# Adding all head dims' products on VectorE, with part of the additions moved to accumulating DMA, in a fused attention and token-MLP kernel

## The chip, the cores and the metric

One core of one Trainium2 chip. The metric is device time in microseconds (us) of one execution. The span of a profile is the time from the first to the last instruction of that execution; device time is a little longer than the span. Every run told below was fast, where not said otherwise.

The engines are named as the profile names them: PE (matmul), PEld (its weight loads), DVE (VectorE), ACT (ScalarE), POOL (GpSimd), SP (the queue that issues most DMAs).

## The reference

The output mixes two branches by a gate per row: `g * a + (1 - g) * b`, with `g = sigmoid(sum(x * gate_w))`, S = 2048 rows and D = 512 columns, bf16.

```python
# branch a: 32 heads of 16 dims; each row attends to 8 rows: itself and 2, 4, ... 14 rows back
logits = einsum("bhsd,bhswd->bhsw", q, kg) * Dh**-0.5      # masked where the row is below 0
attn   = softmax(logits, axis=-1)
o      = einsum("bhsw,bhswd->bhsd", attn, vg);  a = o @ wo
# branch b: an MLP over rows (tokens)
h = layernorm(x);  u = gelu(einsum("bsd,sf->bdf", h, w1) + b1);  y = einsum("bdf,fs->bds", u, w2) + b2
```

## The kernel before

Heads and four groups of head dims lie on the 128 partitions, so a sliding window is a shifted view along the free axis. For each half of the rows (h = 0, 1) DVE multiplies q by eight shifted views of k, for each of four groups `dl` of head dims. The products are summed pairwise on DVE into two buffers; PE then sums the rest with a 0/1 matrix (`RP`, 128 x 32) in one burst of small matmuls that reads both buffers. Softmax runs on DVE and ACT; GpSimd's DMA queue spreads the weights over the head dims ("attention copies"); DVE multiplies by V and adds the eight window places in three steps.

```python
def f_sum(h, b0, b1, with_gate):                 # one burst on PE
    ...                                          # 16 gate matmuls when h == 0
    for wp in range(4):
        for k_, b_ in enumerate((b0, b1)):       # two buffers: 32 matmuls
            for c in range(4):
                ins = e.matmul(ps[32*c:32*c+32, 4+wp, :], lhsT=RP,
                               rhs=sub(PB[b_], 2*wp*HS + c*UT_, [(HS, 2), (1, UT_)]),
                               start=(k_ == 0), stop=(k_ == 1), tile_position=(0, 32*c))
...
for h in range(2):
    for pr in range(2):
        ...                                      # two products into bb[0], bb[1]
        A("dve", tt(PB[bb[0]], PB[bb[0]], PB[bb[1]], ALU.add), ...)
...
for u in range(8):                               # AV, 256 rows each
    A("dve", tt(pv, <V, shifted>, <weights>, ALU.mult), ...)             # 128x8192
    A("dve", tt(pv[:, 0:4], pv[:, 0:4], pv[:, 4:8], ALU.add), ...)       # 128x4096
    A("dve", tt(pv[:, 0:2], pv[:, 0:2], pv[:, 2:4], ALU.add), ...)       # 128x2048
    A("dve", tt(OT[:, u], pv[:, 0], pv[:, 1], ALU.add), ...)             # 128x1024
...
MLPB = [0, 1, 2, 0, 1, 2, 3, 0, 1, 2, 3, 4, 5, 6]    # PSUM bank of each of 14 token-MLP tiles
```

PE's work is one chain in a fixed order: Q, K, V projections; the first MLP product (224 matmuls, "ph2") with the two sum bursts put in; the second MLP product ("ph3") with the output projection of `a` ("wo") added five tiles behind. A list scheduler in the kernel, with its own estimates, orders each engine's instructions when the program is built.

## Time and profile before

| | before |
|---|---|
| device time, median of the first 3 runs | 171.63 us (171.59 to 172.5) |
| profiled execution: device time, span | 170.61 us, 168.5 us |
| PE busy, DVE busy | 161.6 us, 151.9 us |
| PE's first wait of size: for the last V eviction, near 48 us | 0.69 us |
| PE's last wait: for DVE's last AV result | 1.04 us (0.82, see below) |

First the page of the kernel before: the span, then each engine's busy time with its share of the span.

```profile
span 168.5 us, 2085 instructions
...
PE 161.6 (96%) x835; PEld 79.4 (47%) x851; DVE 151.9 (90%) x115; ACT 73.1 (43%) x102; POOL 19.6 (12%) x57
```

The next lines are the waits of before (who waited for whom: us in total, times, longest).

```profile
DVE arena L688 <- DMA arena<-in_A_x_dram: 7.5, 3, 5.2
...
PE ps L841 <- DVE arena L446: 1.0, 1, 1.0
...
DVE arena L446 <- PE ps L719: 0.8, 1, 0.8
PE ps L805 <- ACT arena L449: 0.8, 2, 0.7
```

L841 is the output projection: PE waits for DVE once, at the very end. L688 are the layer norm's statistics, which wait for rows of x at the start. The third line shows that DVE in turn once waits for PE (L719 is the sum burst). The timeline of PE shows where (start us, us, engine, line, shapes; in brackets the idle time before and what ended it):

```profile
9.74 3.40 PE L649 MATMUL ps<-arena 128*128 128x512 bf16 x15
...
48.65 7.08 PE L805 MATMUL ps<-arena 128*128 128x512 bf16 x31 [0.69 <-ACT arena L449]
...
56.53 1.90 PE L719 MATMUL ps<-arena 128*32 128x512 bf16 x32
58.59 6.85 PE L805 MATMUL ps<-arena 128*128 128x512 bf16 x31 [0.16 <-issue]
...
88.23 1.91 PE L719 MATMUL ps<-arena 128*32 128x512 bf16 x32
90.30 1.67 PE L805 MATMUL ps<-arena 128*128 128x512 bf16 x7 [0.16 <-issue]
92.13 10.53 PE L805 MATMUL ps<-arena 128*128 128x512 bf16 x47 [0.15 <-ACT arena L449]
...
159.51 3.62 PE L841 MATMUL ps<-arena 128*128 128x512 bf16 x16
164.18 1.69 PE L841 MATMUL ps<-arena 128*128 128x512 bf16 x11 [1.04 <-DVE arena L446]
```

After the second burst there is one more wait, of 0.15 us for ACT, which evicts the sums. The gap of 0.16 us behind each burst, in which PE seems to wait for nothing, is no wait. This profile holds 851 weight loads but only 835 matmuls: 16 matmuls have no record. Two of them are the first matmuls behind the two bursts (hence x31 and x7, not x32 and x8; the first one's weight load is there, at 58.36 us). In the profile of a1_before, the same program run again (see the experiments), all 851 are there, and the gap is not:

```profile
PE 163.0 (97%) x851; PEld 79.4 (47%) x851; DVE 151.9 (90%) x115; ACT 73.1 (43%) x102; POOL 19.5 (12%) x57
...
56.67 1.90 PE L719 MATMUL ps<-arena 128*32 128x512 bf16 x32
58.51 7.08 PE L805 MATMUL ps<-arena 128*128 128x512 bf16 x32
...
164.09 1.91 PE L841 MATMUL ps<-arena 128*128 128x512 bf16 x12 [0.82 <-DVE arena L446]
```

So from its start to the start of the next matmul a burst takes 1.84 us (56.67 to 58.51). The last wait is 0.82 us: the line of 1.04 above lacks the first of its twelve matmuls. And the durations of DVE's large operations, kept apart by shape (busy us, mean ns of one):

```profile
L446 DVE TENSOR_TENSOR arena<-arena 128x8192 bf16<-128x8192 bf16 x16 | 70.7, 4420 | 1.8 <-DMA arena<-arena 0.9 <-PE ps L719 0.8
L446 DVE TENSOR_TENSOR arena<-arena 128x4096 bf16<-128x4096 bf16 x16 | 36.4, 2288 | 0.2
```

### The profile page before, as it was taken

What the parts mean: (1) busy time and instruction counts of PE and PEld (TensorE: products, weight loads), DVE (VectorE), ACT (ScalarE), POOL (GpSimd) and SP (SyncE); (2) the same over time, 40 slices, a digit from 0 to 9 for tenths busy, and PEclk for the clock granted to TensorE, in tenths of its full rate; (3) what the DMA queues carried; (4) which work ended last, traced back from release to release, by engine and by line L of the source; (5) the groups of instructions that cost most, each with busy time, mean ns of one, the idle gap of its engine ahead of it and who ended that gap; (6) DMA issues with size and microseconds to landing.
All of it is one profiled execution on the core that took longest, in us unless ns stands there. A gap on an engine that the chain in (4) does not pass through costs nothing.

```text
span 168.5 us, 2085 instructions
## 1 busy us (share of the span) xinstructions
PE 161.6 (96%) x835; PEld 79.4 (47%) x851; DVE 151.9 (90%) x115; ACT 73.1 (43%) x102; POOL 19.6 (12%) x57
## 2 busy tenths in 40 slices
PE   6999999999989999999999999999999999999973
PEld 2865555555534444444443444444444444444732
DVE  2609999999999799999979999999999999999981
ACT  3266777666671277656215297000121111111172
POOL 7000000000000000000396000079100000000000
PEclk9999999999999999999999999999999999999999
DMA  5999999910000392995799999999900011000022
GB/s 137 271 247 252 235 321 290 302 66 6 0 0 0 110 302 63 285 286 142 215 218 288 355 275 270 290 243 207 198 31 31 31 46 51 31 31 31 31 91 96
DMA packets 43144, 26.87 MB, mean 159 GB/s; under 512 B 7552, under 2 KB 41984, under 8 KB 43136
## 3 DMA queue, kind: packets, MB, share of 16 engines
q1 hardware_dynamic: 40800, 21.96, 49.9%
q0 software_dynamic: 1632, 4.21, 10.4%
q10 hardware_dynamic: 704, 0.59, 1.1%
q8 instruction: 6, 0.10, 0.3%
q14 instruction: 2, 0.02, 0.0%
HBM read 18.88 MB, written 2.10 MB: 125 GB/s over the span
## 4 chain that ended last, share of the span: by engine, by line
PE 54%; DVE 36%; ACT 4%; issue 3%; DMA 2%; DVEq 0%
DVE arena L446 36%; PE ps L805 24%; PE ps L649 22%; ACT arena L449 3%; PE ps L590 2%; PE ps L719 2%; DMA arena<-in_A_x_dram 2%; PE ps L841 1%; PE ps L569 1%; ACT L901 1%; PE ps L713 1%; PE ps L560 1%; DVE arena L881 0%; DVEq L905 0%; PE ps L779 0%
## 5 line engine op out<-in xcount | busy, mean ns | idle before, releaser
L446 DVE TENSOR_TENSOR arena<-arena 128x8192 bf16<-128x8192 bf16 (+10 forms) x72 | 134.8, 1902 | 3.2 <-DMA arena<-arena 0.9
L832 PE MATMUL ps<-arena 128*128 128x512 bf16 (+1 forms) x234 | 50.0, 366 | 0.2
L805 PE MATMUL ps<-arena 128*128 128x512 bf16 x218 | 48.7, 379 | 1.4 <-ACT arena L449 0.8
L449 ACT ACTIVATE arena<-ps,arena 128x512 bf16<-128x512 f32 (+1 forms) x30 | 21.6, 728 | 65.2 <-PE ps L841 46.6
L449 ACT ACTIVATE arena<-ps 128x512 bf16<-128x512 f32 (+3 forms) x53 | 33.4, 649 | 20.3 <-PE ps L649 10.4
L649 PE MATMUL ps<-arena 128*128 128x512 bf16 x172 | 38.0, 379 | 0.2
L832 PEld LDWEIGHTS ps<-arena 128*128 128x128 bf16 x238 | 23.3, 98 | 25.3
L805 PEld LDWEIGHTS ps<-arena 128*128 128x128 bf16 x224 | 21.5, 98 | 28.2 <-ACT arena L449 1.8
L649 PEld LDWEIGHTS ps<-arena 128*128 128x128 bf16 x176 | 19.8, 113 | 17.7
L771 POOL DMA_DIRECT2D arena<-arena x32 | 16.4, 517 | 98.3 <-DVE arena L446 98.3
L688 DVE BATCH_NORM_STATS2 arena<-arena 128x6 f32<-128x512 bf16 x16 | 10.0, 682 | 7.5 <-DMA arena<-in_A_x_dram 7.5
L841 PE MATMUL ps<-arena 128*128 128x512 bf16 (+1 forms) x66 | 15.5, 366 | 1.1 <-DVE arena L446 1.0
L901 ACT ACT_TABLE_LOAD x9 | 11.5, 1283 | 2.4 <-issue 2.3
L841 PEld LDWEIGHTS ps<-arena 128*128 128x128 bf16 x68 | 6.6, 98 | 8.2 <-DVE arena L446 1.3
L449 ACT ACTIVATE arena<-arena 128x16 f32<-128x16 f32 (+5 forms) x10 | 6.8, 679 | 5.2 <-DVE arena L446 5.1
L702 DVE TENSOR_SCALAR arena<-arena 128x512 bf16<-128x512 bf16 x16 | 5.3, 413 | 0.0
L590 PE MATMUL ps<-arena 128*128 128x256 bf16 x32 | 3.8, 273 | 0.0
L719 PE MATMUL ps<-arena 128*32 128x512 bf16 x64 | 3.8, 380 | 0.0
L590 PEld LDWEIGHTS ps<-arena 128*128 128x128 bf16 x32 | 3.4, 114 | 0.4 <-DVE arena L580 0.4
L543 PE MATMUL ps<-arena 128*128 128x512 bf16 x5 | 2.3, 628 | 1.1 <-POOL arena L455 1.1
L719 PEld LDWEIGHTS ps<-arena 128*32 128x32 bf16 x64 | 1.6, 97 | 1.9 <-issue 0.4
L881 DVE TENSOR_SCALAR arena<-ps,arena 128x256 bf16<-128x256 f32 x1 | 0.5, 544 | 2.0 <-PE ps L841 2.0
(36 smaller groups left out, 15.3 us busy)
## 6 DMA issues: line engine op xcount, KB each, us to landing
arena<-in_B_w_dram SPq DMA_DIRECT2D x7, 1024.0 KB, 8.3
arena<-in_B_w_dram SPq DMA_DIRECT2D x8, 896.0 KB, 7.9
arena<-arena POOLq DMA_DIRECT2D x32, 128.0 KB, 4.3
out_dram<-arena SPq DMA_DIRECT2D x15, 128.0 KB, 1.7
arena<-in_A_x_dram SPq DMA_DIRECT2D x3, 512.0 KB, 4.3
arena<-in_A_wqkv_dram SPq DMA_DIRECT2D x2, 512.0 KB, 5.9
arena<-in_A_wo_dram SPq DMA_DIRECT2D x1, 512.0 KB, 8.7
arena<-in_A_x_dram SPq DMA_DIRECT2D x2, 128.0 KB, 3.4
```

What stands on the lines that cost most here:

```text
L446: return lambda e: e.tensor_tensor(out=o_, in0=a_, in1=b_, op=op_)
L449: return lambda e: e.activation(out=o_, in_=i_, func=f_, **kw)
L590: ins = e.matmul(ps[:, dl, hb * 256:hb * 256 + 256], lhsT=sub(WQKV, dt * 3 * D + dl, [(4, 128)]), rhs=XT[:, dt, hb * 256:hb * 256 + 256], ...
L649: ins = e.matmul(ps[:, bank, :], lhsT=sub(WQKV, dt * 3 * D + tn * D + dl, [(4, 128)]), rhs=XT[:, dt, sb * 512:(sb + 1) * 512], start=(dt = ...
L688: A("dve", (lambda t_: lambda e: e.bn_stats(out=ST6[:, t_, :], in_=X[:, t_, :]))(t), 0.67, reads=["x%d" % t], writes=["st%d" % t], name="s ...
L702: A("dve", (lambda t_: lambda e: e.tensor_scalar(out=X[:, t_, :], in0=X[:, t_, :], scalar1=col(RSTD, t_), scalar2=col(NMR, t_), op0=ALU.mu ...
L719: ins = e.matmul(ps[32 * c:32 * c + 32, 4 + wp, :], lhsT=RP, rhs=sub(PB[b_], 2 * wp * HS + c * UT_, [(HS, 2), (1, UT_)]), start=(k_ == 0), ...
L771: prev = sch.dma("pool", (lambda d_, s_: lambda e: e.dma_start(d_, s_))(dst, src), 131072, ds, issue=1.0, reads=["att%d" % h], writes=["av ...
L805: ins = e.matmul(ps[:, bank, :], lhsT=W1W[:, (ft // 2) % 3, st, 128 * (ft % 2):128 * (ft % 2) + 128], rhs=X[:, st, :], start=(st == 0), st ...
L832: ins = e.matmul(ps[:, bank, 0:c1 - c0], lhsT=W2S[i // 2][:, ft, 128 * (i % 2):128 * (i % 2) + 128], rhs=UT[:, ft, c0:c1], start=(ft == 0) ...
L841: ins = e.matmul(ps[:, bank, 0:c1 - c0], lhsT=OT[:, i // 2, dl, 128 * (i % 2):128 * (i % 2) + 128], rhs=WO[:, dl, c0:c1], start=False, sto ...
L901: e.preload_act_table_set(want)
```

## The change

The intent: let each sum burst read one buffer, so that PE has half as many small matmuls; DVE then has to add all four head-dim groups, and to make room on DVE, five additions (two of the pair additions of the first half, three of the eight first additions of AV) are done by DMAs that accumulate into their destination. The rest makes that fit: half-buffers laid out flat (s_ = 0, 1), a third AV buffer, another home for one W2 tile and for the output staging, plain loads of x ahead of the transposing ones, two of the first Q evictions on DVE, the W1 tiles 1 and 2 held back until the second accumulation has landed, the 32 attention copies merged into 8, and a new order of PSUM banks for the MLP.

```diff
             for k_ in range(1, 4):
+                ld_x(4 * k_, 4)
                 ld_xt(k_)
-                ld_x(4 * k_, 4)
...
-            evac(0, dl, 0, dl)
+            evac(0, dl, 0, dl, "act" if dl % 2 == 0 else "dve")
...
                 for wp in range(4):
-                    for k_, b_ in enumerate((b0, b1)):
-                        for c in range(4):
-                            ins = e.matmul(... rhs=sub(PB[b_], ...), start=(k_ == 0), stop=(k_ == 1), ...)
+                    for c in range(4):
+                        ins = e.matmul(... rhs=sub(PB[b0], ...), start=True, stop=True, ...)
...
+            def qaddd(x_, y_, s_, h=h):
+                o_, i_ = (sub(PB[b_], s_ * 4096, [(1, 4096)]) for b_ in (x_, y_))
+                qkd[h, s_] = sch.dma("pool", lambda e: e.dma_start(o_, i_, accum_op=ALU.add, max_dma_last_dim=4096), ...)
+            for s_ in range(2):
+                qk(0, bb[0], s_)
+                qk(1, bb[1], s_)
+                (qaddd if h == 0 else qadd)(bb[0], bb[1], s_)
+            ...
+            for s_ in range(2):
+                qadd(bb[0], bb[2], s_)
...
-                for dhi in range(4):             # 16 attention copies of 128 KB per half
+                src = psub(ATT[h], 32 * c, 32, 0, [(0, 4), (1, NW * UT_)])     # 4 of 512 KB
...
+        late_dep[0] = [qkd[0, 1]]
+        ld_w1(1); ld_w1(2)
...
+        AVD = (3, 4, 5)                          # AV units whose first addition is a DMA
...
-        MLPB = [0, 1, 2, 0, 1, 2, 3, 0, 1, 2, 3, 4, 5, 6]
+        MLPB = [1, 2, 0, 1, 2, 0, 3, 1, 2, 0, 3, 1, 2, 0]
```

(Priorities, buffer names and the ring of banks of ph3 change too.)

## The prediction

> **What bounds it now.** The page gives PE 161.6 us busy of 168.5 (96%), DVE 151.9 (90%), full granted clock. The two run neck and neck. The chain of waits runs on PE until about 92 us, then through ACT (log eviction, table load, exp) into DVE, which from 99.7 to 163.9 us never pauses (timeline). PE has little slack: it reaches the last output projection at 163.1 and waits 1.04 us for it (waits of PE on DVE). A gain needs both engines shortened.
>
> **Removed, added, moved (durations from the trace).**
> - PE: each sum burst goes from 32 small matmuls to 16. A burst takes 1.87 us (88.30 to 90.17 in the chain), so about 0.9 us less each, 1.8 us in all.
> - PE: the first token-MLP matmul waits 0.69 us for the last V eviction; the new bank order starts elsewhere: about 0.6 us less.
> - DVE, QK: before, 8 half-size products (2.29 us), 4 full-size products and 4 full-size additions (4.42 us): 53.7 us. After: 26 half-size operations, 59.5 us: +5.8 us.
> - DVE, AV: three half-size additions go to DMA: -6.9 us. Two Q evictions come over from ACT: about +1.4 us. So DVE's total is unchanged (+0.3 us).
> - DVE gains at the start: it idles 5.25 us, 7.6 to 12.8 us, waiting for x rows (waits). With plain loads ahead of the transposing ones the statistics start near 10.4 us. I count 3 us less idle: DVE finishes near 161.
> - Cost at the start: the second DVE Q eviction stands behind four statistics (4 x 0.62 us); PE's small bias transposes want its bank at 13.1 us and would wait about 0.5 us.
> - DMA: five accumulating transfers of 1 MB source each. [...] My estimate: the 32 software-queue copies move 4.2 MB in 10.4% of 16 engines' span, about 240 GB/s[...]. The order of instructions leaves about 9 us before DVE needs the second QK one and the first AV one. This is the tightest spot.
>
> **Critical path.** PE's arrival at the last projection: 163.1 - 1.8 - 0.6 + 0.5 = 161.2 us. DVE's finish about 161. The 1.04 us wait mostly vanishes: the end moves from 168.5 to about 165.5 us. Off 171.63 that is 168.6; I add a little for slips of the accumulating DMAs.
>
> **Prediction: 168.8 us, 80% range 167.5 to 171.0.** Faster by over 2%: 0.27; within 2%: 0.70; slower by over 2%: 0.03.
>
> **What would show it.** Sum bursts near 0.9 us each; no eviction wait near 48 us; DVE busy near 152 us with less idle before 13 us; layer norm done near 30 us, not 33; sum burst 0 near 54 and burst 1 near 92 us; accumulating DMAs landing in 8 to 10 us; the last PE wait under 0.5 us.
>
> **What would make it wrong.** Accumulating DMAs of 12 us or more: DVE stalls before its fourth products and the delayed AV additions, sum burst 0 holds PE, and the gain shrinks to 1 us or none. Their traffic delaying weight loads (two W1 loads now wait for the second accumulation). Transposing loads landing later and stalling projections near 13 or 21 us. On the good side: if the evictions and loads at the start cost PE nothing, 167.5.

With them the forecast for 1 MB came to about 9 to 11 us from issue to landing, where "What would show it" says 8 to 10: the author's estimate.

## The result, and the profile after

The changed kernel took 166.95 us (median of 4 runs, 166.47 to 167.41) against 171.61 (4 runs). The ratio is 0.9721, 95% interval 0.9683 to 0.9758: faster by 2.8%. A ratio here is formed from the fast runs of both kernels in the same rounds, so it is not quite the ratio of the medians quoted. The time lies 0.55 us below the predicted range, and over the 2% line that had been given a chance of 0.27.

| | before | after |
|---|---|---|
| device time, median | 171.61 us | 166.95 us |
| span of the profiled execution | 168.5 us | 165.3 us |
| PE busy, DVE busy | 161.6, 151.9 us | 159.8, 150.9 us |
| K projections start on PE | 9.74 us | 10.54 us |
| sum bursts start | 56.53 and 88.23 us | 54.74 and 92.30 us |
| last DVE result for PE | 163.9 us | 159.2 us |

The page of the changed kernel:

```profile
span 165.3 us, 1999 instructions
...
PE 159.8 (97%) x803; PEld 78.8 (48%) x819; DVE 150.9 (91%) x124; ACT 69.7 (42%) x98; POOL 13.7 (8%) x38
```

The waits of the changed kernel that answer to those shown of before (the line numbers have moved: L687 are the statistics, L892 the output projection, L717 the sum burst):

```profile
DVE arena L687 <- DMA arena<-in_A_x_dram: 3.7, 4, 1.8
...
PE ps L567 <- DMA arena<-in_A_x_dram: 0.8, 2, 0.7
...
DVE arena L445 <- DMA arena<-arena: 0.2, 1, 0.2
```

PE no longer waits for DVE anywhere. DVE waits for PE at the start (2.1 us, for the Q projections that it now evicts) and before the last instruction, and no more at the bursts. What is left of PE's waits after its first microsecond is one for an x tile at the start (L567). All five accumulating DMAs together make DVE wait 0.2 us. The timeline of PE of the changed kernel:

```profile
10.54 3.40 PE L648 MATMUL ps<-arena 128*128 128x512 bf16 x15
...
48.59 5.34 PE L856 MATMUL ps<-arena 128*128 128x512 bf16 x23
...
54.74 1.04 PE L717 MATMUL ps<-arena 128*32 128x512 bf16 x16
55.71 7.08 PE L856 MATMUL ps<-arena 128*128 128x512 bf16 x31
...
92.30 1.05 PE L717 MATMUL ps<-arena 128*32 128x512 bf16 x16
93.30 7.07 PE L856 MATMUL ps<-arena 128*128 128x512 bf16 x31
...
157.22 5.35 PE L892 MATMUL ps<-arena 128*128 128x512 bf16 x27
```

The wait before the MLP is gone (48.59). The first burst takes 0.97 us to the start of the next matmul (54.74 to 55.71), about half as long as before. The output projections run through to the end without a wait. DVE's large operations:

```profile
L445 DVE TENSOR_TENSOR arena<-arena 128x4096 bf16<-128x4096 bf16 x31 | 69.5, 2287 | 0.1
L445 DVE TENSOR_TENSOR arena<-arena 128x8192 bf16<-128x8192 bf16 x8 | 35.2, 4420 | 0.0
```

The 31 half-size operations add up to 69.5 us busy, not to 31 times their mean (70.9): neighbours overlap by some 0.05 us on average. And the accumulating DMAs of 1 MB each, issued at L742 (QK) and L825 (AV), first the two QK ones (time from issue to landing: shortest, median, longest), then the three AV ones, which were issued 4.3 us apart:

```profile
DMA to landing us min/median/max: 7.9/7.9/8.0
```

```profile
DMA to landing us min/median/max: 8.6/10.3/12.5
```

**The sum, from the K projections' start to PE's end.** Before, PE's stretch runs from 9.74 to 165.87 us (164.18 + 1.69), after from 10.54 to 162.57 us (157.22 + 5.35): 156.1 against 152.0, so 4.1 us less. (In both profiles the record of the first of these matmuls is missing, which moves both starts alike, by 0.22 us.) I count every part from the start of one matmul to the start of the next, in profiles or stretches where no record is missing. Without a wait this step is 0.22 us, but the record of a matmul is 0.38 us long, so neighbours overlap: a wait costs 0.16 us more than the idle time that the profile shows. The two bursts give 1.7 us (1.84 each in a1_before, 0.97 here). The eviction wait gives 0.86 (shown: 0.69) and the last wait 0.98 (shown in a1_before: 0.82). Two stops of PE in the MLP's first product give 0.49: 0.31 behind the second burst (shown: 0.15), and 0.18 near 72 us, where one step takes 0.39 us and no wait is shown. Together that is about 4.05. Which part of the change removed these two stops no run separates. The span fell by only 3.2 us because this one profile of the changed kernel started its K projections 0.8 us later. That the profile's span of 165.3 us agrees with the predicted 165.5 is thus partly luck, and the experiments had to separate the two.

### The profile page after: what moved, and what is told of

It is laid out like the page before. It is cut to its first block, busy times and chain, and to the rows that moved or that the text cites. A ratio compares the mean times of both kernels' runs of the same rounds, so it can differ in the third digit from the quotient of the medians.

```text
span 165.3 us, 1999 instructions
## 1 busy us (share of the span) xinstructions
PE 159.8 (97%) x803; PEld 78.8 (48%) x819; DVE 150.9 (91%) x124; ACT 69.7 (42%) x98; POOL 13.7 (8%) x38
## 4 chain that ended last, share of the span: by engine, by line
PE 93%; DMA 3%; issue 1%; ACTq 1%; DVE 0%
PE ps L856 29%; PE ps L883 29%; PE ps L648 23%; PE ps L892 8%; DMA arena<-in_A_x_dram 3%; PE ps L588 2%; PE ps L717 1%; PE ps L712 1%; ACTq L487 1%; DVE arena L932 0%; PE ps L567 0%; PE ps L797 0%; PE ps L661 0%; PE ps L663 0%; PE ps L662 0%
## 5 line engine op out<-in xcount | busy, mean ns | idle before, releaser
L445 DVE TENSOR_TENSOR arena<-arena 128x4096 bf16<-128x4096 bf16 (+9 forms) x79 | 131.9, 1720 | 1.2 <-DMA arena<-arena 0.2
L448 ACT ACTIVATE arena<-ps 128x512 bf16<-128x512 f32 (+3 forms) x51 | 32.7, 647 | 20.0 <-PE ps L648 11.1
L892 PE MATMUL ps<-arena 128*128 128x512 bf16 (+1 forms) x66 | 15.3, 366 | 0.1
L687 DVE BATCH_NORM_STATS2 arena<-arena 128x6 f32<-128x512 bf16 x16 | 10.1, 682 | 3.7 <-DMA arena<-in_A_x_dram 3.7
L785 POOL DMA_DIRECT2D arena<-arena x8 | 4.4, 563 | 75.2 <-DVE arena L445 75.2
L892 PEld LDWEIGHTS ps<-arena 128*128 128x128 bf16 x68 | 6.7, 98 | 7.2
L825 POOL DMA_DIRECT2D arena<-arena x3 | 3.6, 1200 | 17.7 <-DVE arena L445 17.7
L742 POOL DMA_DIRECT2D arena<-arena x2 | 2.5, 1234 | 30.3 <-DVE arena L698 21.6
## 6 DMA issues: line engine op xcount, KB each, us to landing
arena<-arena POOLq DMA_DIRECT2D x8, 512.0 KB, 11.2
```

What stands on the lines that cost most here:

```text
L445: return lambda e: e.tensor_tensor(out=o_, in0=a_, in1=b_, op=op_)
L448: return lambda e: e.activation(out=o_, in_=i_, func=f_, **kw)
L687: A("dve", (lambda t_: lambda e: e.bn_stats(out=ST6[:, t_, :], in_=X[:, t_, :]))(t), 0.67, reads=["x%d" % t], writes=["st%d" % t], name="s ...
L785: prev = sch.dma("pool", (lambda d_, s_: lambda e: e.dma_start(d_, s_))(dst, src), 524288, sch.dsem("av%d_%d" % (h, c)), issue=1.0, reads= ...
L825: sch.dma("pool", (lambda o_, i_: lambda e: e.dma_start(o_, i_, accum_op=ALU.add, max_dma_last_dim=4096))(pw(0, 4), pw(4, 4)), 1800000, sc ...
L892: ins = e.matmul(ps[:, bank, 0:c1 - c0], lhsT=OT[:, i // 2, dl, 128 * (i % 2):128 * (i % 2) + 128], rhs=WO[:, dl, c0:c1], start=False, sto ...
```

## The experiments

All had five rounds. Numbers are medians, with the ratio to the kernel before in the same rounds. Where "pinned" is said, each engine's instruction order was fixed to that of the kernel named, since the scheduler otherwise moves other work as well. I checked that pinning alone gives instruction for instruction the same program; that check is not among the runs on record. "PE's stretch" is the one of the sum above, from the first recorded K projection to PE's end.

### a1_before: the kernel before, run again

No edit.

> The kernel before, unchanged, run again so that each timed execution also shows its span. Open question: the profile of before had a span of 168.5 us and a device time of 170.61, while its timed runs gave 171.5 to 172.5; the changed kernel's profile (165.3, 166.99) agrees with its timed runs. Theory A (span varies): ordinary executions of before have spans of 169.4 to 170.5, that is the profile on record was a fast draw. Theory B (overhead outside the span): spans stay at 168.5 and time minus span is about 3.1 us for before against 1.7 us for after.

Measured: 170.89 us (6 runs); the 11 runs of before beside it gave 171.46 us. Spans ran from 168.6 to 169.8 us; time minus span was 2.1 to 2.3 us, mean 2.2. So both theories are half right. Executions of before differ by over 1 us in span, and the profile (168.5) was one of the shortest. Besides, before spends about 0.45 us more outside the span than the changed kernel (mean 1.7 us).

### a2_oldload: the old load order in the changed kernel, scheduler free

```diff
-                ld_x(4 * k_, 4)
                 ld_xt(k_)
+                ld_x(4 * k_, 4)
```

> The changed kernel with the loads of before (transposing load first, plain rows of x after it). Theory: the new load order makes the fourth x tile land late and costs PE 0.65 to 0.8 us at 7.4 us; undone, PE starts the K projections at 9.7 instead of 10.5 us, and since DVE finished 2 us before PE needed its last output, DVE's later start costs at most part of that: time 166.2 to 166.8, a ratio to before of about 0.968 to 0.971. Rival (the early loads are worth what they were meant for, because DVE is a co-bottleneck): DVE's layer norm ends at 33 instead of 31 us, PE waits at a sum burst or at the end, time 167.5 to 169.

Measured: 168.84 us, ratio 0.9841 (0.9801 to 0.9881). My theory of the late x tile was not borne out: the wait for it is gone here, but PE's K projections started at 10.31 us all the same (10.32 in the changed kernel, once its missing first record is allowed for), since the first Q projections ran slowly (below). The main loss was elsewhere, in a wait of PE for the last of the first MLP's weight tiles, since the scheduler had moved other things:

```profile
PE ps L856 <- DMA arena<-in_B_w_dram: 1.6, 1, 1.6
```

What does vary at the start shows in two profiles' timelines, the same eight matmuls first in this run, then in the changed kernel's:

```profile
5.70 1.71 PE L588 MATMUL ps<-arena 128*128 128x256 bf16 x8
```

```profile
5.53 1.06 PE L588 MATMUL ps<-arena 128*128 128x256 bf16 x8
```

Eight matmuls of 256 columns take 1.71 us in one and 1.06 in the other. Why the eight ran more slowly in one is not shown: the granted clock of both runs reads 1.0 as a mean of the whole run. And other profiles lost time at the start to first DMAs that landed late (0.65 us in the changed kernel's profile, for x), so the slow pace explains only part of the spread of spans.

### a3_dveadds: the five accumulations back on DVE

```diff
-                (qaddd if h == 0 else qadd)(bb[0], bb[1], s_)
+                qadd(bb[0], bb[1], s_)
-        AVD = (3, 4, 5)
+        AVD = ()
```

(The held-back W1 loads then wait for the matching DVE addition.)

> The changed kernel with all five accumulating DMAs replaced by the same additions on VectorE. Theory: DVE gets 5 x 2.29 = 11.4 us more, its end moves from 159.2 to about 170.6 and PE waits for it: time about 175 to 177, slower than before by about 2 to 3%. Rival (PE bounds the kernel and DVE has room): time within 1 us of the changed kernel, 167 to 168.

Measured: 177.57 us, ratio 1.0365 (1.0335 to 1.0395): 10.6 us more than the changed kernel and slower than before, as the theory had it; the time is 0.6 us above the stated range. The timeline of PE of this run shows the wait:

```profile
169.60 3.53 PE L895 MATMUL ps<-arena 128*128 128x512 bf16 x12 [6.75 <-DVE arena L445]
```

Without the accumulating DMAs the change would be a loss: PE's saving needs room on DVE, and they make it. The twelve matmuls after the wait also take 3.53 us, where the same twelve take 1.91 us in a1_before after a wait of 0.82 us. The granted clock of this run was 1.00 from 150 to 160 us and 0.77 in the mean from 160 to 175 us, the stretch that holds the wait and the twelve matmuls. After its wait of 6.75 us PE restarted slowly here. So some 1.6 us of the loss (3.53 against 1.91) are slow matmuls, not waiting. The scheduler was free in this run.

### a4_twobuf: bursts from two buffers again, without the final pair additions

```diff
-                    for c in range(4):
-                        ins = e.matmul(... rhs=sub(PB[b0], ...), start=True, stop=True, ...)
+                    for k_, b_ in enumerate((b0, b2)):
+                        for c in range(4):
+                            ins = e.matmul(... rhs=sub(PB[b_], ...), start=(k_ == 0), stop=(k_ == 1), ...)
...
-            for s_ in range(2):
-                qadd(bb[0], bb[2], s_)
```

> The changed kernel with the sum bursts reading two buffers again (no final pair additions on VectorE: 9.2 us less for DVE; 32 more small matmuls on PE: 1.8 us more). Theory (PE's stream alone bounds the changed kernel): bursts 1.8 us each again, time 168.5 to 169.0. Rival (DVE still bounds): DVE is 9 us shorter, so the time falls below 166.

Measured: 172.35 us over all six runs, two of them slow; the four fast ones had 170.82 to 172.97 and a ratio of 1.002 (0.9974 to 1.0066). Both theories missed. DVE was shorter, so the accumulating DMAs came earlier (120.0, 124.4 and 128.7 us instead of 127.7, 132.1 and 136.4) and ran beside the last weight loads. Of the last three loads of 896 KB one took 21.8 us to land, and the last, issued at 120.2 us, took 27.7; the last two have a median of 32.0, which puts the other near 36.3. The median of all such loads of the changed kernel is 10 us. Four attention copies, issued from 106.4 us on, landed there too, after 11.2 us in the median. The last load landed near 147.9 us (120.2 + 27.7), and an output DMA, issued behind it on the same queue at 131.8 us, at 148.3. The chain of waits of this run's profile (start us, us, what):

```profile
131.78 16.49 DMA out_dram<-arena
...
148.36 0.79 ACT arena L448
...
149.19 1.04 PE ps L882 x2
```

One output DMA of 128 KB took 16.5 us, its staging buffer was not free for ACT, and PE waited 4.6 us. Only this profile, of a slow run, shows this chain; what held the loads up is not shown, and the median time is not explained in amount. The time of this run does not measure the burst; b6_doubleburst does, with the rest held still.

### b4_after: the changed kernel, run again

No edit.

> The changed kernel, unchanged, run again for spans and the start of PE. The first four experiments showed that executions of before differ in span (168.6 to 169.8 us) and that in some profiles PE's first projection matmuls run at half pace until about 7.1 us and in others not. Theory: both kernels' spans spread over about 1 us for this reason, and the changed kernel's spans here run from 164.6 to 165.8 with a median near 165.2; time minus span 1.7 us. Ratio to before 0.970 to 0.974.

Measured: 166.95 us, ratio 0.9738 (0.9693 to 0.9782); spans 164.8 to 166.0 us, against 168.6 to 170.8 for before in the same rounds; time minus span 1.74 us. As expected, but for the longest span (165.8 was expected). Comparing shortest spans (168.6 and 164.8) gives 3.8 us, medians (169.1 and 165.2) 3.9 us. That agrees with the 4.1 us of the sum above, and not with the 3.2 us between the two profiles.

### b6_doubleburst: each small sum matmul issued twice, all else pinned

```diff
-                    for c in range(4):
+                    for c in (0, 1, 2, 3, 0, 1, 2, 3):
```

> The changed kernel with each of its 32 sum matmuls issued twice (the second overwrites the first with the same values), all engine orders pinned, so only PE gets 32 more small matmuls, as many as before; DVE, ACT and DMA have the same work in the same order. Theory (PE's in-order stream bounds the changed kernel from start to end): +1.7 to 1.8 us, time 168.6 to 168.8. Rival (a burst's length hides behind waits on DVE, as it did in part before): less than 0.8 us more.

Measured: 168.92 us, ratio 0.9846 (0.9802 to 0.9889), so 2.0 us more than the changed kernel. The timeline of PE:

```profile
54.87 1.90 PE L722 MATMUL ps<-arena 128*32 128x512 bf16 x32
56.93 6.85 PE L861 MATMUL ps<-arena 128*128 128x512 bf16 x31 [0.16 <-issue]
```

The gap of 0.16 us is again the missing record of the first matmul behind the burst (x31; 835 matmuls and 851 weight loads in this profile). Set 0.22 us earlier, that matmul starts near 56.71: the burst takes 1.84 us to it, 0.87 more than in the changed kernel. PE's stretch is 153.75 us (10.67 to 164.42) against 152.03, so 1.72 us more for both bursts. The medians of the spans differ by 1.75 us (166.95 and 165.2). The 2.0 us in time hold one run of six that spent 3.2 us outside its span, and the two ratios do not separate 2.0 from 1.7. So what PE's chain gains or loses here comes out in full, and a halved burst is worth 0.86 us: the prediction's "about 0.9 us less each" was right.

### b5_oldload_pin: the old load order in the changed kernel, all else pinned

The edit of a2_oldload, with the orders of the changed kernel.

> The changed kernel with the old load order alone, all other orders pinned to those of the changed kernel (in a2_oldload the scheduler had moved other work too, and PE lost 1.6 us to a late W1 tile). DVE's statistics of rows 4 to 7 wait about 2 to 2.5 us longer. Theory (DVE has about 2 us of room at the end, PE bounds): 0 to 0.7 us slower than the changed kernel, since the second accumulating DMA and sum burst 0 come later by 1.5 to 2.5 us and burst 0 was ready before PE only just. Rival (the early loads delay the fourth x tile and cost PE): faster by 0.5 us or more.

Measured: 168.3 us, ratio 0.9818 (0.9769 to 0.9867): 1.35 us slower than the changed kernel, more than either theory said. PE waited 0.65 us for the DVE eviction that stands behind the four statistics, and 0.28 us more for a weight load behind the second burst. PE's stretch is 1.23 us longer. The first of the two waits:

```profile
PE ps L653 <- DVE arena L629: 0.6, 1, 0.6
```

So the early rows of x matter in the changed kernel also because an eviction that PE needs stands behind them in DVE's order; with that order pinned, part of this loss is made by the pinning.

### b1_avmerge_pin: before, with the 32 attention copies merged into 8, other engines pinned

```diff
-                for dhi in range(4):
-                    ...                          # 128 KB each
+                src = psub(ATT[h], 32 * c, 32, 0, [(0, 4), (1, NW * UT_)])
```

> The kernel before with its 32 attention-copy DMAs merged into 8 (this part of the change alone; engine orders pinned). Question: time minus span is 2.0 to 2.3 us for before and 1.7 for every kernel made from the changed one. Theory: the number of DMAs and their semaphores sets what an execution spends outside the span, so here it is 1.7 to 1.8 with the span unchanged at 168.6 to 169.8: time 170.4 to 171.3, ratio about 0.997. Rival (it comes from something else, such as the first or last part of the program): 2.1 as before.

Measured: 173.24 us, ratio 1.0099 (1.005 to 1.0149). Slower, by 0.5 to 1.5%: DVE's first AV product, which in before waits 0.85 us for its copy, waits longer here for the merged one (the first sixteen copies of 128 KB landed 7.3 us after issue in the median in before; the first four of 512 KB after 10.6 us in the changed kernel):

```profile
DVE arena L451 <- DMA arena<-arena: 3.1, 1, 3.1
```

In the changed kernel the same merging is hidden, for DVE has eight half-size operations (2.29 us each) of the second half to do between the softmax and that product, which starts at 91.1 us; the last of the first four copies, issued at 75.6 us, landed after at most 14.1 us. Time minus span was 1.9 us, between the two values.

### c1_evqswap: the two DVE Q evictions of the changed kernel in the order that the prediction assumed, pinned

```diff
-  DVE order: ... 'ext1_0', 'evq3_0', 'st4', 'st5', 'st6', 'st7', 'evq1_0', ...
+  DVE order: ... 'ext1_0', 'evq1_0', 'st4', 'st5', 'st6', 'st7', 'evq3_0', ...
```

(`evq` are the two Q evictions, `st` the statistics; bank 3 is that of `evq3_0`.)

> The changed kernel with the two Q evictions on DVE swapped in its order (bank 1 first, bank 3 behind the four statistics), all else pinned. That is the order that the prediction had assumed, with a PE stall of 0.5 us at the small bias transposes, which read into bank 3. Theory (the prediction had the right mechanism but the wrong order; in the changed kernel bank 3 is evicted first, so the stall never comes): PE waits 0.4 to 0.8 us at the bias transposes near 14 us and the time is 0.4 to 0.8 us longer than the changed kernel's 166.95. Rival (the stall would be hidden): no difference (below 0.2 us).

Measured: 167.02 us, ratio 0.975 (0.9711 to 0.9788). The profile has the stall, but of 0.30 us:

```profile
13.62 0.18 PE L666 MATMUL ps<-arena 14*128 14x14 bf16 x1 [0.30 <-DVE arena L629]
```

PE's stretch is 0.36 us longer than the changed kernel's (152.39 against 152.03). In the time it is below what these rounds can tell from nothing (0.1 us in the medians; 0.3 against c2_avsplit, run in the same rounds, with the intervals overlapping). So the step in the prediction had named a real stall, for an order that the changed kernel does not have, and had it too large.

### c2_avsplit: the changed kernel with 32 attention copies, pinned

The edit of b1_avmerge_pin the other way round.

> The changed kernel with its 8 attention-copy DMAs of 512 KB split into the 32 of 128 KB of before, all orders pinned. Time minus span was 2.1 to 2.4 us for before, 1.7 to 1.8 for the changed kernel, and 1.8 to 2.1 for before with the copies merged. Theory (what an execution spends outside the span goes with the number of GpSimd DMAs or their semaphores): 2.0 to 2.2 here, the span within 0.2 us of 165.2, time about 167.2 to 167.4. Rival (it is something else in the program): 1.7 to 1.8, time as the changed kernel's.

Measured: 166.70 us, ratio 0.9725 (0.9695 to 0.9755), time minus span 1.74 us. PE's stretch is the changed kernel's (152.02 us). The theory fell: the number of copies is not what before spends outside the span. That 0.45 us stays unexplained. Merging the copies gains nothing either.

### c3_bank: before with the new bank order of the MLP's first product alone, pinned

```diff
-        MLPB = [0, 1, 2, 0, 1, 2, 3, 0, 1, 2, 3, 4, 5, 6]
+        MLPB = [1, 2, 0, 1, 2, 0, 3, 1, 2, 0, 3, 4, 5, 6]
```

(The first eleven places are those of the changed kernel; the last three stay as in before.)

> The kernel before with the new bank order of the token-MLP's first matmuls alone (PE no longer waits 0.69 us for the last V eviction). Theory (PE and DVE are coupled: DVE waits 0.84 us for sum burst 0 near 58 us, so what PE gains before it, DVE gains too): 0.5 to 0.7 us faster than before. Rival (DVE alone sets the end in before): no gain, the last PE wait grows from 1.0 to 1.7 us.

Measured: 170.37 us, ratio 0.9933 (0.9899 to 0.9966), between 0.6 and 1.7 us faster. The timeline of PE:

```profile
47.94 7.07 PE L810 MATMUL ps<-arena 128*128 128x512 bf16 x31
...
55.82 1.90 PE L724 MATMUL ps<-arena 128*32 128x512 bf16 x32
...
163.47 1.68 PE L846 MATMUL ps<-arena 128*128 128x512 bf16 x11 [1.05 <-DVE arena L451]
```

The wait at 48 us is gone, the burst starts 0.7 us earlier, and the end comes 0.7 us earlier with the same last wait (1.05 us as the profile shows it, again with eleven of twelve records). As this execution started its K projections 0.15 us later than the profile of before, PE's stretch is 0.87 us shorter. DVE, which had waited for the burst, moved along with PE. The two engines are coupled at the burst, as the theory said; "DVE alone sets the end" is wrong.

### c4_bankloads: c3_bank with the new load order as well, pinned

```diff
+                ld_x(4 * k_, 4)
                 ld_xt(k_)
-                ld_x(4 * k_, 4)
```

> The kernel before with the new bank order and the new load order (plain rows of x first), other orders pinned. DVE starts its statistics about 2.5 us earlier. Theory (in before's order DVE's early time is lost again in its wait for sum burst 0, which has a fixed place in PE's stream): within 0.3 us of c3_bank. Rival (the early loads shorten the DVE chain to the end): 0.8 us or more faster than c3_bank, and PE's last wait gone.

Measured: 170.36 us, ratio 0.9941 (0.9909 to 0.9972): the same as c3_bank. DVE started early and gave it back. These are its waits for PE in c4_bankloads:

```profile
DVE arena L674 <- PE ps L669: 1.6, 1, 1.6
...
DVE arena L451 <- PE ps L724: 1.0, 1, 1.0
```

DVE waits 1.0 us for the burst, where c3_bank shows no such wait of size. In before's order an earlier DVE is worth nothing.

## Why the prediction was wrong

The direction and most steps were right; the gain was too small. Predicted 168.8, measured 166.95 us.

What held: layer norm done near 30 us (30.9); bursts at 54 and 92 us (54.7 and 92.3); accumulating DMAs landing in 8 to 10 us (7.9 and 8.0 for QK; 8.6 to 12.5 for AV, so one was past the 12 us that were to do harm), with DVE waiting 0.2 us; PE's last wait under 0.5 us (none), with DVE's finish, predicted at 161, at 159.2; the balance "DVE's total is unchanged" (-1.0 us measured, where +0.3 was predicted: 31 half-size operations overlap by 1.4 us in all).

What failed was the sum for PE's arrival, "163.1 - 1.8 - 0.6 + 0.5 = 161.2 us". With most of the 1.04 us wait it takes 3.0 us off PE's path, where the profiles show 4.1. The terms, and what stood outside the sum:

1. "Would wait about 0.5 us" at the bias transposes: this cost was not there. The changed kernel's DVE evicts bank 3 first, so PE finds it free. I took the order of the two evictions for granted; the listing shows two like-looking rows. With the assumed order PE loses 0.36 us (c1_evqswap).
2. Two stops of PE in the MLP's first product, together 0.49 us, were not counted: 0.31 behind the second burst and 0.18 near 72 us. The changed kernel has neither.
3. "About 0.6 us less" for the bank order: it was worth 0.87 us of PE's stretch (c3_bank; its time says 0.6 to 1.7). The shown wait of 0.69 us leaves out 0.16 us by which matmuls overlap when nothing holds them.
4. "About 0.9 us less each, 1.8 us in all" for the bursts was right: 0.86 each, 1.72 in all (b6_doubleburst).
5. Time outside the span, 2.2 us before and 1.74 us after, was taken as unchanged. It gave 0.45 us more. Why is open.
6. The 0.2 us added "for slips of the accumulating DMAs" was not needed.

That is 0.5 + 0.49 + 0.27 - 0.08 + 0.45 + 0.2 = 1.83 us, of the 1.85 us by which the time was missed. So close an agreement is partly luck, as executions of one kernel spread by over 1 us. The profile would not have told: its span of 165.3 us seems to confirm 165.5, because that execution lost 0.8 us more at the start than the profile of before.

The stated reason for a gain, "needs both engines shortened", holds only in part. c3_bank shortened PE alone, ahead of the sum burst where DVE waits for it, and was faster. An earlier DVE alone was worth nothing (c4_bankloads against c3_bank). Moving the additions back to DVE costs 10.6 us (a3_dveadds), and while DVE has room, what PE saves comes out in full (b6_doubleburst).

## What to carry to other kernels

When two engines are both above 90% busy, list where each waits for the other: in this kernel a saving before such a meeting moved both engines (0.87 us, c3_bank), and an earlier start of the one that waits there was given back (a wait of 1.0 us, c4_bankloads). An addition of 1 MB that a DMA does beside the engines freed the vector engine here (five of them back on it cost 10.6 us, a3_dveadds), and landed in 7.9 to 12.5 us; look at what else is on the queues then, since in one slow run (a4_twobuf), with such additions and copies beside them, three weight loads took 22 to 36 us to land instead of 10, and an output 16.5. Before you read a short gap as a wait, compare the number of matmuls with that of weight loads: a missing record looks like one (0.16 us here, with 835 of 851 matmuls recorded). Compare spans of several executions, not of one profile each, before you call a sum confirmed: the 11 runs of before beside c3_bank had 168.4 to 170.1 us.
